# A gated mix of a recurrent memory attention and a full attention: paired weight tails, and attention steps set between the first products

## The chip, the cores and the metric

The kernel runs on one core of a Trainium2 chip, as one launch. The metric is device time in microseconds (us). TensorE is called PE, VectorE DVE, ScalarE ACT, GpSimd POOL; SP is the engine whose queue issues most of the transfers ("sync").

## The reference, cut to what matters

Two attentions over the same 2048 tokens of 576 features are mixed by a gate. A works in 64 segments of 32 tokens, each with 8 memory rows ahead of it. The memory of a segment is what the segment before gave out, so the segments of A form one long chain. B is an ordinary attention of 32 heads of 18 features over all tokens, without a mask, and depends on nothing in A.

```python
def A(x, mem, Wq, Wk, Wv, Wo):              # H, Dh = 32, 128; M, seg = 8, 32
    for s in range(64):
        h = concatenate([mem, x[:, 32*s:32*s+32]], axis=1)      # 40 rows
        q, k, v = h @ Wq, h @ Wk, h @ Wv                        # 576 -> 32 x 128 each
        scores = where(mask, q @ k.T * Dh ** -0.5, -1e9)
        o = (softmax(scores) @ v) @ Wo                          # 4096 -> 576
        mem = o[:, :8]
        outs.append(o[:, 8:])

def B(x, wqkv, wo):                         # 32 heads of 18
    q, k, v = split(x @ wqkv)
    return softmax(q @ k.T * 18 ** -0.5) @ v @ wo

g = sigmoid((x * gate_w).sum(-1))
out = g * A + (1 - g) * B
```

All tensors are bfloat16.

## The kernel before

The order of work on every engine is the order of the program. There are three parts: an opening (x is transposed, B's q, k and v are projected to DRAM, A's weights are loaded), the 64 segments, and a closing part (B's output product and the gate).

B's attention is cut into 512 steps (8 groups of four heads, 4 blocks of 512 queries, 16 blocks of 128 keys). A step is one PE part, `B` in the order strings below, and one exponential on ACT, `E`. The score tile `sb` has one buffer of four PSUM banks, so the scores of a step wait for the exponential of the one before.

```python
for j in range(4):                                   # scores: four row groups of PE, 32x128
    nc.tensor.matmul(sb[:, j, :], lhsT=kc[32*j:32*j+32, o:o+P],
                     rhs=qch[gq][32*j:32*j+32, :], tile_position=(32*j, 0), ...)
...                                                  # values of the step before: four column groups, 128x32
nc.scalar.activation(out=before, in_=sb, func=ACT.Exp, scale=scale_b)      # E, 128 x 2048
```

q and k of B lie in DRAM in the form in which the steps want them, 32 rows for a head of 18, so that one load brings a group. The 14 rows of padding are zeroed by transfers of their own, and a block of projected rows is stored head by head.

```python
qtd = dpool.tile([GB, P, S], BF16, name="qtd")       # ktd the same
def load_kv(g, kc):
    loads.dma_start(out=kch[g, kc][:, :], in_=ktd[g, :, kc*KC*P:(kc+1)*KC*P])
    ...
def store_qk(blk, groups):                           # one transfer for each head (or part of one) in the block
    while f < (blk + 1) * P: ... nc.sync.dma_start(out=(qtd, ktd)[which][h // 4, r:r+n, :], in_=stgs[blk][...])
```

The 576 features are four chunks of 128 and a tail of 64. The tails of a weight lie in two halves of one tile, one in each half of the partitions; the other half of the moving or stationary rows is zero, so a tail is multiplied as a full chunk of 128 rows. A segment's projection takes 32 tokens as stationary data and four column groups of PE at a time:

```python
def project(x, w, b, k):                             # Q0 Q1 K0 K1 V0 V1
    for c in range(NF + 1):                          # NF = 4; the fifth is the tail
        for j in range(4):
            rw, cc = w_slice(w, c, (2*(j//2)+b)*1024 + (j%2)*512, 512)
            nc.tensor.matmul(pv[32*j:32*j+32, :], lhsT=ht[:, cc, :], rhs=rw,
                             start=(c == 0), stop=(c == NF), tile_position=(0, 32*j))
```

A segment has 40 rows, `ht` has 32 columns: the last 8 tokens of the segments don't depend on the memory as queries, keys and values, and are projected for 16 segments at once (`last_tokens`, 24 pieces a group: q, k and v by eights). Group 0 is done ahead of the segments; groups 1 to 3 fill places `F0` to `F2` in segments 0 to 47, where every fourth segment uses these places for its group's output product instead. From segment 48 on there is none of it left.

Each segment's work is put in order by a string; names are steps, `B` and `E` halves of B's steps, `/` and `:` parts of B's divisions on DVE. `Q0` is a product, `cQ0` its copy out of PSUM, `tq0` transposes, `pq0` their copy, `S` scores, `x` their exponential, `n` the mask, `p` sums, `l` and `r` the reciprocal by logarithm and exponential, `m` the division, `w` and `o` values and their copy, `a` the output product, `h` and `g` its two bfloat16 halves, `f` and `ht` the fold into the next segment's `ht`.

```python
ORDERS = {
    7: "Q0 cQ0 K0 B E : cK0 / K1 tq0 tk0 pq0 V0 cK1 B E : pk0 Q1 S0 cV0 v0 cQ1 x0 tk1 n0 B E : ...",
    8: "Q0 B E : V0 cQ0 K0 cV0 v0 B / cK0 E : tq0 pq0 Q1 tk0 pk0 cQ1 B / E : S0 K1 tq1 x0 cK1 B ...",
}
eights = GB * NQC * NKB + 1 - done[0] - 7 * n_seg    # done: steps taken before the segments
width = 8 if s >= n_seg - eights else 7
```

In the opening, the steps are taken after whole products:

```python
def between(cost):
    spare[0] += cost
    if spare[0] >= 1.8:
        spare[0] -= 1.8
        b_advance(1)
for kb in range(NKB):
    project_vb(1, kb, 3)                             # second half of B's values, nine tiles in turn
for blk in (1, 6, 2, 7, 3, 8):
    for t in range(NQC):
        project_qk(blk, t, 0)                        # five matmuls of 512
        between(1.1)
    store_qk(blk, range(GB))
...                                                  # wo is loaded
for i, _ in enumerate(last_tokens(0, 1 << 30)):      # group 0: 24 pieces, four staging tiles
    if i % 2:
        between(1.1)
```

Of the kernel before, what the change touches and what calls it, by code (L numbers as in the profile page):

```python
# [16 lines left out]
def kernel(  # L17
# [64 lines left out]
    qtd = dpool.tile([GB, P, S], BF16, name="qtd")  # L82
    ktd = dpool.tile([GB, P, S], BF16, name="ktd")
# [11 lines left out]
    def weights(name):  # L95
        return (
            aw1.tile([P, NF, HD], BF16, name=name + "_m"),
            aw1.tile([P, HD // 2], BF16, name=name + "_t"),
        )

    wv, wq, wk = weights("wv"), weights("wq"), weights("wk")

    def load_weights(w, src):
        w2 = src.rearrange("d h e -> d (h e)")
        for c in range(NF):
            yield nc.gpsimd.dma_start(out=w[0][:, c, :], in_=w2[c * P:(c + 1) * P, :])
        for two in range(2):
            yield nc.gpsimd.dma_start(
                out=w[1][TL * two:TL * two + TL, :],
                in_=w2[NF * P:Dm, two * (HD // 2):(two + 1) * (HD // 2)],  # L110
            )

    def w_slice(w, c, f0, n):

        if c < NF:
            return w[0][:, c, f0:f0 + n], c
        f1 = f0 % (HD // 2)
        return w[1][:, f1:f1 + n], NF + f0 // (HD // 2)
# [17 lines left out]
    KC = 4  # L136
    last_stage = []
# [51 lines left out]
    def b_steps():  # L189


        kch, vch, qch = {}, {}, {}

        def load_kv(g, kc):
            kch[g, kc] = bint.tile([P, KC * P], BF16, name="kch", bufs=6)
            loads.dma_start(out=kch[g, kc][:, :], in_=ktd[g, :, kc * KC * P:(kc + 1) * KC * P])
            vch[g, kc] = bint.tile([P, KC * P], BF16, name="vch", bufs=6)
            first_loads[:] = [loads.dma_start(
# [4 lines left out]
        def load_q(i):  # L203
            if i < GB * NQC:
                g, qc = divmod(i, NQC)
                qch[i] = bint.tile([P, QC], BF16, name="qch", bufs=3)
                loads.dma_start(out=qch[i][:, :], in_=qtd[g, :, qc * QC:(qc + 1) * QC])
# [54 lines left out]
    loads, first_loads = nc.sync, []  # L262
# [30 lines left out]
    xlbs = {}  # L293
# [6 lines left out]
    def last_tokens(q, share, k=None):  # L300
# [3 lines left out]
        stage = (lambda: seg2.tile([P, 512], BF16, name="tm", bufs=4)) if share else (  # L304
            lambda: fil.tile([P, 512], BF16, name="vl")
        )
        store = nc.sync if share else nc.gpsimd
        xlb = xlbs.pop(q)
        for b in range(HD // 512):
            pv = bank(k[0], [P, 512], FP32, "pv")  # L310
            for c in range(NF + 1):
                rw, cc = w_slice(wv, c, b * 512, 512)
                nc.tensor.matmul(pv[:, :], lhsT=xlb[:, cc, :], rhs=rw, start=(c == 0), stop=(c == NF))  # L313
            vl = stage()
            yield
            copy_out(vl[:, :], pv[:, :], share)
            store.dma_start(out=vld[q * P:(q + 1) * P, b * 512:(b + 1) * 512], in_=vl[:, :])
            yield
        for w, dstd in ((wq, qld), (wk, kld)):
            for b in range(H // 4):  # L320
# [16 lines left out]
                if w is wk and b == H // 4 - 1:  # L337
                    load_xlb(q + 1)
                yield

# [34 lines left out]

    zt = pw.tile([P, S], BF16, name="stg", bufs=3)
    nc.vector.memset(zt[0:32 - DhB, :], 0.0)

    def pads(t, g):
        return t[g].rearrange("(j r) s -> j r s", r=32)[:, DhB:32, :]  # L380

# [33 lines left out]
    def project_qk(blk, t, share):  # L415
# [3 lines left out]
        for c in range(NF + 1):  # L419
# [6 lines left out]
            )  # L426
        copy_out(stgs[blk][:, t * QC:(t + 1) * QC], pq[:, :], share)

    def store_qk(blk, groups):
        f = blk * P  # L430
        while f < (blk + 1) * P:
            which, h, e = f // Dm, f % Dm // DhB, f % DhB
            n = min(DhB - e, (blk + 1) * P - f)
            r = 32 * (h % 4) + e
            if h // 4 in groups:
                nc.sync.dma_start(
                    out=(qtd, ktd)[which][h // 4, r:r + n, :], in_=stgs[blk][f - blk * P:f - blk * P + n, :]
                )
            f += n
# [18 lines left out]

    FIRST = (0, 4, 5)
    pieces = [(w, src) for w, src in ((wv, A_Wv), (wq, A_Wq), (wk, A_Wk))]  # L460
    pieces = (d for w, src in pieces for d in load_weights(w, src))
    for t in range(NQC):
        for n in range(4 * t, 4 * t + 4):
# [6 lines left out]
        if t == 0:  # L470
            load_xlb(0)
            for r in range(8):
                nc.gpsimd.dma_start(out=pads((qtd, ktd)[r // 4], 0)[r % 4], in_=zt[0:32 - DhB, :])
        for blk in FIRST:
            project_qk(blk, t, 2)
        if t == NQC - 1:
            for blk in FIRST:
                store_qk(blk, (0,))
        for kb in range(4 * t, 4 * t + 4):
            project_vb(0, kb, 2)  # L480

# [6 lines left out]
    load_first()  # L488
    ready.extend([first_loads[-1]] * 2)
# [19 lines left out]


    spare = [0.0]

    def between(cost):
        spare[0] += cost
        if spare[0] >= 1.8:
            spare[0] -= 1.8
            b_advance(1)

    for blk in FIRST:
        store_qk(blk, range(1, GB))  # L520
    for kb in range(NKB):
        project_vb(1, kb, 3)
    for blk in (1, 6, 2, 7, 3, 8):
        for t in range(NQC):
            project_qk(blk, t, 0)
            between(1.1)
        store_qk(blk, range(GB))
# [5 lines left out]
    for q in range(4):  # L533
        in_turn(
            nc.gpsimd.dma_start(
                out=wo[:, 8 * q:8 * q + 8, :], in_=A_Wo[8 * q:8 * q + 8].rearrange("h e d -> e h d")
            )
        )
    fix = actx.enter_context(tc.tile_pool(name="fix", bufs=1))
    seg2 = actx.enter_context(tc.tile_pool(name="seg2", bufs=2))  # L540


    def pad(g):
        for t in (qtd, ktd):
            nc.gpsimd.dma_start(out=pads(t, g), in_=pads(t, 0))

    pad(1)


# [582 lines left out]
```

The softmax here doesn't subtract the row's maximum and nothing guards it: scores larger than these inputs give would overflow.

## Time and profile before

| | |
|---|---|
| time, median of three runs | 1616.8 us (1615.98 to 1621.42) |
| span of the profiled execution | 1613.9 us |
| first product of the first segment | 174.5 us |
| PE, DVE, ACT, POOL busy | 91%, 59%, 71%, 21% of the span |
| PE on the chain that ended last | 69% |
| DMA, moved in all | 114.39 MB |

The busy share of PE counts each matmul from its start to its modelled end. As matmuls are pipelined, 379 ns of a matmul of 512 overlap with its neighbours, and the true cost of one is read from the distance of starts. The chain that ended last goes back from the last instruction to what released it, and names the engine that set the time at each moment; DMA has 4% of it, ACT and DVE 11% each. The most frequent line on it is the segments' projection with 27%.

### The profile page before, as it was taken

How to read it: one execution, taken by the hardware profiler on the slowest of the kernel's cores; microseconds unless marked ns; L12 is line 12 of the kernel's file. 1: busy time of each engine (PE TensorE's matmuls, PEld its weight loads, DVE VectorE, ACT ScalarE, POOL GpSimd, SP SyncE). 2: the span in 40 equal slices, each digit the busy share in tenths (PEclk: the TensorE clock that was granted, in tenths of full speed). 3: DMA queues.
4: the chain of work that ended last, by engine and by line, in shares of the span. 5: the costliest groups of instructions: out<-in, count | busy, mean ns of one | idle time of the engine just before them, and what ended most of it. 6: DMA issues, size and time to landing. Idle time of an engine off the chain costs nothing.

```text
span 1613.9 us, 57766 instructions
## 1 busy us (share of the span) xinstructions
PE 1476.7 (91%) x25082; PEld 782.0 (48%) x25082; DVE 960.0 (59%) x2355; ACT 1139.8 (71%) x981; POOL 338.4 (21%) x731
## 2 busy tenths in 40 slices
PE   6598899999999999999999999999999989998997
PEld 3434444555454444555454445555554444444445
DVE  2233666666566666666566666666666656565656
ACT  2165577777677767777677777777777777788774
POOL 6311211213131031302121211212121212120131
PEclk9899999999999999999999999999999999999999
DMA  7788322212122121212122121212221121211125
GB/s 200 235 291 290 100 65 64 49 42 52 45 50 53 32 53 38 61 36 49 43 43 60 38 50 40 57 39 45 51 53 35 30 48 34 45 34 35 29 59 162
DMA packets 209865, 114.39 MB, mean 71 GB/s; under 512 B 159491, under 2 KB 197251, under 8 KB 208019
## 3 DMA queue, kind: packets, MB, share of 16 engines
q1 hardware_dynamic: 188971, 58.40, 16.1%
q0 software_dynamic: 19696, 50.02, 9.9%
q8 instruction: 196, 3.21, 0.9%
q10 hardware_dynamic: 944, 2.29, 0.4%
q14 instruction: 58, 0.48, 0.1%
HBM read 60.94 MB, written 36.10 MB: 60 GB/s over the span
## 4 chain that ended last, share of the span: by engine, by line
PE 69%; ACT 11%; DVE 11%; DMA 4%; issue 2%; SPq 1%; POOL 1%; DVEq 0%; ACTq 0%; POOLq 0%
PE pvv L755 27%; ACT etb L257 9%; PE sb L238 8%; PE ob L222 7%; PE pt L782 5%; PE pv L326 4%; PE psh L800 3%; PE acc L643 3%; PE pso L838 3%; PE pv L313 2%; DVE hl L657 2%; PE pq L420 2%; DVE hl L654 2%; DVE ot L850 2%; ACT rq L830 2%
## 5 line engine op out<-in xcount | busy, mean ns | idle before, releaser
L257 ACT ACTIVATE etb<-sb 128x2048 bf16<-128x2048 f32 x512 | 959.6, 1874 | 341.9 <-PE sb L238 341.1
L767 DVE CAST tm<-pvv 128x512 bf16<-128x512 f32 x384 | 264.4, 689 | 175.1 <-PE pvv L755 174.2
L755 PEld LDWEIGHTS <-ht 128*32 128x32 bf16 x7680 | 185.8, 97 | 183.7 <-DVE ht L891 14.1
L238 PE MATMUL sb<-qch,kch 32*128 32x512 bf16 x2048 | 203.2, 386 | 38.5 <-ACT etb L257 36.7
L222 PE MATMUL ob<-etb,vch 128*32 128x512 bf16 x2048 | 205.9, 392 | 3.9 <-DVE tq L159 3.9
L850 DVE CAST ot<-pso 128x320 bf16<-128x320 f32 x256 | 120.7, 488 | 104.2 <-PE pso L838 99.9
L643 PE MATMUL acc<-wo,ot 128*32 128x384 bf16 (+1 forms) x4096 | 159.7, 291 | 5.4 <-DVE ot L850 3.3
L755 PE MATMUL pvv<-wq_m,ht 128*32 128x512 bf16 x2048 | 134.2, 382 | 13.0 <-DVE ht L891 8.3
L755 PE MATMUL pvv<-wk_m,ht 128*32 128x512 bf16 x2048 | 134.9, 384 | 0.0
L755 PE MATMUL pvv<-wv_m,ht 128*32 128x512 bf16 x2048 | 134.3, 382 | 0.0
L643 PEld LDWEIGHTS <-ot 128*32 128x32 bf16 x4096 | 105.2, 98 | 46.5 <-DVE ot L850 12.8
L700 POOL DMA_DIRECT2D a_dram<-rl x186 | 92.6, 506 | 162.4 <-DVE rl L695 143.3
L238 PEld LDWEIGHTS <-kch 32*128 32x128 bf16 x2048 | 61.2, 91 | 128.5 <-issue 107.9
L857 POOL COPY otl<-ot 128x256 bf16<-128x256 bf16 x64 | 25.9, 405 | 445.6 <-DVE ot L850 445.6
L222 PEld LDWEIGHTS <-vch 128*32 128x32 bf16 x2048 | 52.9, 93 | 120.6 <-issue 116.0
L782 PE MATMUL pt<-ident,tm 128*128 128x128 bf16 x1024 | 96.8, 221 | 0.8 <-DVE tm L767 0.8
L790 DVE COPY kt<-pt 128x512 bf16<-128x512 bf16 x128 | 54.0, 422 | 69.4 <-PE pt L782 69.0
L838 PE MATMUL pso<-et,v_sb 64*128 64x40 bf16 x2048 | 81.4, 178 | 14.9 <-DVE hll L657 4.7
L838 PEld LDWEIGHTS <-v_sb 64*128 64x128 bf16 x2048 | 62.8, 93 | 62.4 <-issue 49.5
L654 DVE CAST hl<-acc 128x384 bf16<-128x384 f32 (+1 forms) x128 | 57.9, 452 | 58.1 <-PE acc L643 57.8
L782 PEld LDWEIGHTS <-tm 128*128 128x128 bf16 x1024 | 57.8, 98 | 67.0 <-issue 49.4
L826 ACT ACTIVATE lt<-pss 128x320 f32<-128x320 f32 x128 | 56.0, 438 | 43.2 <-PE pss L822 32.8
(141 smaller groups left out, 1847.4 us busy)
## 6 DMA issues: line engine op xcount, KB each, us to landing
v_sb<-tm SPq DMA_DIRECT2D x512, 32.0 KB
wo<-in_A_Wo_dram POOLq DMA_DIRECT2D x4, 1152.0 KB, 9.7
wv_m<-in_A_Wv_dram POOLq DMA_DIRECT2D x4, 1024.0 KB, 8.0
wq_m<-in_A_Wq_dram POOLq DMA_DIRECT2D x4, 1024.0 KB, 9.1
wk_m<-in_A_Wk_dram POOLq DMA_DIRECT2D x4, 1024.0 KB, 8.0
xl<-qld SPq DMA_DIRECT2D x64, 64.0 KB
xl<-kld SPq DMA_DIRECT2D x64, 64.0 KB
v_sb<-vld SPq DMA_DIRECT2D x128, 32.0 KB
```

The source lines that it names most:

```text
L222: nc.tensor.matmul(ob[32 * j:32 * j + 32, :], lhsT=vc[:, o + 32 * j:o + 32 * j + 32], rhs=et4[:, j, :], start=(kb == 0), stop=(kb == NKB - 1),
L238: nc.tensor.matmul(sb[:, j, :], lhsT=kc[32 * j:32 * j + 32, o:o + P], rhs=qch[gq][32 * j:32 * j + 32, :], start=True, stop=True, tile_posi ...
L257: nc.scalar.activation(out=before[:, :, :], in_=sb[:, :, :], func=ACT.Exp, scale=scale_b)
L326: nc.tensor.matmul(pv[:, o:o + P], lhsT=lw, rhs=xlb[:, cc, :], start=(c == 0), stop=(c == NF))
L643: nc.tensor.matmul(acc[32 * j:32 * j + 32, 0:d1 - d0], lhsT=o[:, h, 0:CT], rhs=wo[:, h, d0:d1], start=(b == 0 and i == 0), stop=(b == 1 an ...
L654: nc.vector.tensor_copy(out=hl[:, 0, d0:d1], in_=acc[:, 0:d1 - d0])
L700: eng.dma_start(out=rows4[m, seg - LO:seg, i * n:(i + 1) * n], in_=rl[32 * i + m * LO:32 * i + (m + 1) * LO, :],)
L755: nc.tensor.matmul(pv[32 * j:32 * j + 32, :], lhsT=ht[:, cc, :], rhs=rw, start=(c == 0), stop=(c == NF), tile_position=(0, 32 * j),)
L767: nc.vector.tensor_copy(out=sbt[x][:, :], in_=ps[x][:, :])
L782: nc.tensor.transpose(out=pt[:, which, :, :, :].rearrange("p j (u i) t -> p j u i t", i=4)[:, :, :, i, :], in_=sbt[x][:, i * Dh:(i + 1) * Dh],
L838: nc.tensor.matmul(pso[:, i * L:(i + 1) * L], lhsT=v_sb[64 * jj:64 * jj + 64, b * 1024 + i * Dh:b * 1024 + (i + 1) * Dh], rhs=et[64 * jj:6 ...
L850: nc.vector.tensor_copy(out=ot[:, j * HG:(j + 1) * HG, :].rearrange("p h t -> p (h t)"), in_=ps["o", b, jj][:, 0:W8],)
```

## The change

It does six things. The tails of the weights are laid out so that the tails of two products lie in different halves of the partitions, and three steps `T0`, `T1` and `T2` multiply them in pairs, each with 64 rows, in eight tiles of PE at once; the first four chunks stay as they were. The last 16 segments, which have no last-token work, keep whole projections and the old eight-step order. The other segments have new orders, and those with eight steps are the first ones now. Last-token values and the sums of the softmax are computed in four column groups. q and k of B lie densely in DRAM, without padding, and are loaded head by head into tiles that were zeroed once; blocks are stored whole. In the opening, steps are set between the matmuls of a product, last-token pieces alternate with products, part of the weights is loaded earlier and `wo` later.

The purpose is to give PE less to do where it is full, and to keep it supplied in the opening.

```diff
-    qtd = dpool.tile([GB, P, S], BF16, name="qtd")
-    ktd = dpool.tile([GB, P, S], BF16, name="ktd")
+    qkd = dpool.tile([2 * Dm, S], BF16, name="qkd")
...
+    wv, wq, wk = weights("wv", 1), weights("wq", 1), weights("wk", 0)     # which half holds the odd quarters
...
+        def load_heads(eng, t, f, t0):
+            for j in range(4):
+                eng.dma_start(out=t[32 * j:32 * j + DhB, :], in_=qkd[f + j * DhB:f + (j + 1) * DhB, t0:t0 + QC])
...
-    def store_qk(blk, groups):
-        ... (a transfer for each head)
+    def store_qk(blk):
+        nc.sync.dma_start(out=qkd[blk * P:(blk + 1) * P, :], in_=stgs[blk][:, :])
...
+    for t in range(NQC):
+        for _ in range((0, 1, 1, 2)[t]):
+            next(pieces)                        # weight pieces; order wq, wk, wv (was wv, wq, wk)
...
+    first_tokens = last_tokens(0, 1 << 30)
+    def some_tokens():
+        for _ in range(2):
+            next(first_tokens, None)
+        between(1.1)
-    for kb in range(NKB):
+    for kb in range(NKB // 2):
         project_vb(1, kb, 3)
-    for blk in (1, 6, 2, 7, 3, 8):
+    for i, blk in enumerate((1, 6, 2, 7, 3, 8)):
         for t in range(NQC):
             project_qk(blk, t, 0)               # calls between(.22) after each matmul; a step at 1.7
-            between(1.1)
-        store_qk(blk, range(GB))
+            if i > 0:
+                some_tokens()
+            else:
+                for kb in range(NKB // 2 + 2 * t, NKB // 2 + 2 * t + 2):
+                    project_vb(1, kb, 3)
+        store_qk(blk)
...
+        def project_tails(two):
+            two = [(x, w, b, begin(x)) for x, w, b in two]
+            for j in range(4):
+                for x, w, b, first in two:
+                    t, r = w_tail(w, columns(b, j), 512)
+                    nc.tensor.matmul(ps[x][32 * j:32 * j + 32, :], lhsT=ht[TL * r:TL * r + TL, NF + r, :],
+                                     rhs=t[TL * r:TL * r + TL, :], start=first, stop=(not first),
+                                     tile_position=(TL * r, 32 * j), ...)
...
+        if not whole:
+            step("T0", project_tails, (("Q0", wq, 0), ("K0", wk, 0)))
+            step("T1", project_tails, (("Q1", wq, 1), ("K1", wk, 1)))
+            step("T2", project_tails, (("V0", wv, 0), ("V1", wv, 1)))
...
     ORDERS = {
-        7: (as above)
+        7: """
+        Q0 T0 B E : cQ0 K1 K0 B Q1 cK0 T1 tq0 cK1 tk0 pk0 E : pq0 B E : cQ1 V0 S0 x0 T2 cV0 v0 B V1 n0
+        p0 tq1 tk1 E : cV1 v1 B l0 E : pk1 / pq1 F1 S1 x1 r0 cF1 F2 n1 m0 p1 l1 w01 B cF2 w00 r1 o01 m1
+        o00 w11 o11 w10 a00 o10 ol E : a01 h0 a10 a11 B F0 g0 f0 h1 g1 E : cF0 f1 ht0 ht1 og oh / /
+        """.split(),
         8: """
+        Q0 B T0 K1 E : / cQ0 T1 cK1 B Q1 E : K0 B V0 cQ1 cK0 T2 tk0 E : tq0 B V1 / cV0 v0 pk0 E : pq0
+        tk1 tq1 cV1 v1 pq1 S0 pk1 B x0 / F1 E : n0 S1 p0 x1 cF1 n1 l0 F2 p1 r0 m0 w00 B cF2 l1 o00 r1 F0
+        m1 w01 w11 cF0 o01 E : w10 o11 o10 ol a00 B a01 E : a10 h0 a11 B g0 h1 f0 g1 ht0 f1 ht1 E : og
+        oh
+        """.split(),
+        0: (the old 8, with whole projections)
...
-    eights = GB * NQC * NKB + 1 - done[0] - 7 * n_seg
+    wides = GB * NQC * NKB + 1 - done[0] - 7 * n_seg - SG
...
-        width = 8 if s >= n_seg - eights else 7
+        width = 8 if s < wides else 7 if s < n_seg - SG else 0
```

`SG` is 16. The order of the PSUM banks is new as well for widths 7 and 8.

## The prediction

> **What bounds the kernel now.** I read the granted clock first (0.986 over the span, 0.99 to 1.00 in the segments: no throttling to explain), then the forty slices, the stages, the order of TensorE's work inside one segment, and last the waits of the opening. The stages come from the four-stage table; its borders are the first and last writes of the memory columns of `ht` (197.3 and 1558.0) and the first segment products (174.5).
>
> ```profile
> PE   6598899999999999999999999999999989998997
> 0.00:174.50 174.50, 130.37 (x1110) 72.33 (x1110) 62.08 (x118) 72.97 (x82) 53.42 (x106) 0.93 0.77 244
> 197.30:787.90 590.60, 555.50 (x10044) 297.04 (x10044) 374.84 (x930) 419.47 (x352) 121.71 (x266) 0.99 0.21 50
> 787.90:1212.60 424.70, 409.67 (x7274) 213.76 (x7274) 266.24 (x668) 326.73 (x266) 86.83 (x190) 1.00 0.21 47
> 1212.60:1558.00 345.40, 314.98 (x5742) 160.38 (x5743) 210.17 (x537) 274.55 (x225) 55.87 (x130) 1.00 0.17 35
> ```
>
> After the borders and the length the columns are the busy time of PE, weight loads, DVE, ACT and POOL, then clock, DMA share and GB/s. Rows two to four are 27 segments of seven attention steps (21.87 us each), 19 of eight with last-token work beside them (22.35) and 16 of eight without it (21.59). PE is busy 94%, 96% and 91% of them, ACT 71%, 77% and 79%, DVE about 62%. So PE's queue sets the length of the first two kinds. The third has less PE work and is hardly shorter: there the segment's own chain and the exponentials count too. What PE does is seen in the order of time:
>
> ```profile
> 700.38 1.05 PE L755 MATMUL pvv<-wq_m,ht 128*32 128x512 bf16 x16
> 701.25 0.39 PE L755 MATMUL pvv<-wq_t,ht 128*32 128x512 bf16 x4
> 701.47 1.04 PE L755 MATMUL pvv<-wk_m,ht 128*32 128x512 bf16 x16
> 702.33 0.39 PE L755 MATMUL pvv<-wk_t,ht 128*32 128x512 bf16 x4
> 702.65 0.40 PE L238 MATMUL sb<-qch,kch 32*128 32x512 bf16 x4
> 702.98 0.40 PE L222 MATMUL ob<-etb,vch 128*32 128x512 bf16 x4
> 703.20 1.04 PE L755 MATMUL pvv<-wk_m,ht 128*32 128x512 bf16 x16
> ```
>
> Read starts, not durations. Four column-tiled matmuls of 512 start together and occupy PE for 0.22 us (701.25 to 701.47; the fifth chunk, a tail of 64 rows padded with zeros, costs as much as a full one). From the tails to the scores it is 0.32 us (702.33 to 702.65), from scores to values 0.33, from values to the next products, which keep the tile shape, 0.22. A change of tile shape thus costs 0.1 us.
>
> The opening waits for data instead:
>
> ```profile
> PE pvb L447 <- DVE xn L291: 16.0, 1, 16.0
> PE sb L238 <- ACT etb L257: 5.0, 10, 0.5
> PE pvb L447 <- DVE stg L291: 4.4, 1, 4.4
> PE pq L420 <- DMA wb<-in_B_wqkv_dram: 3.9, 4, 2.0
> PE ob L222 <- DVE tq L159: 3.9, 1, 3.9
> PE ptm L616 <- DVE ht L598: 3.2, 1, 3.2
> ```
>
> The 16 us are from 62.9 to 78.84: the value tiles can't be reused before their stores land, and these stand in the sync queue behind the many small stores of q and k by head, while A's weights fill the DMA engines:
>
> ```profile
> 66.00:150.00 84.00, 62.63 (x438) 27.14 (x438) 29.47 (x49) 40.68 (x24) 13.98 (x24) 0.88 0.88 296
> 63.44 2.85 SPq L436 DMA_DIRECT2D qtd<-stg  x8
> 66.34 2.75 SPq L436 DMA_DIRECT2D ktd<-stg  x7
> 69.32 5.61 SPq L455 DMA_DIRECT2D vgd<-xn  x5
> ```
>
> **What the Trainium skill says.** "TensorEngine Tiling (Array Packing)", section Key Properties: changing the tiling mode drains TensorE. The trace agrees, with 0.1 us. "TensorE: Matmul & The Clock Gate", section Part 3: Packing small matmuls: tiles that differ in rows and columns run together, at about 4 ns more per tile. The trace agrees for four tiles; no run yet shows eight tiles of 64x32, on which the pairing rests. "DMA: Bandwidth & Descriptors", section Issuing engines are not separate DMA queues: sync and gpsimd transfers share 16 engines, so a second issuing queue saves issue time only. The 0.88 share above, with gpsimd's weights and sync's stores together, agrees; hence it helps that fewer stores are issued and that `wo` comes later, not who issues.
>
> **The change, part by part.** First the counts. Attention steps before the segments: formerly 48 calls of 1.1 against 1.8, so 29; now 24x5 calls of 0.22 and 24 of 1.1, together 52.8 against 1.7, so 31. The rest of 513 gives 513-31-448-16 = 18 wide segments at the start, then 30 of seven steps, then 16 of the old eight-step order with whole projections (formerly 28 and 36).
>
> (a) Tails. Each segment had six tail groups of four, 6x0.215 = 1.29 us. T0, T1 and T2 do eight matmuls each in the two row halves; if those run together that is 3x0.215 = 0.645. Saved 0.645 in 48 segments.
>
> (b) Shape changes. Going through the order strings and counting neighbours of different shape (B counts as two shapes), a seven-step segment had 28 to 31 and has 27 to 29, though each T adds up to two, because T sits next to a step, the sums are now column-tiled, and last-token values keep the 128x32 shape. An eight-step one had 32 to 34 and has 30 to 33. Over the four kinds of segments in a group (two last-token fills in three of them, group output in one) that is about 2 and 2.5 changes, 0.2 and 0.25 us.
>
> (c) New waits. I walked the new orders with the rows' durations: 0.69 for a copy out of `pvv`, 0.42 for `qt` and `kt`, 1.88 for an exponential, 0.43 to 0.47 for the three small activations. The first steps are 2.25 to 2.35 us apart on PE, just what scores plus exponential need; the second half waits for the exponentials about as now. The walk gave some 20.4 and 21.1 us, but such a walk leaves out small queue gaps, so I credit only (a) and (b): 21.87-0.85 = 21.02, and 22.35-0.9 = 21.45. The last 16 keep their order and gain only 0.1: 21.49.
>
> (d) Opening, now 174.5 us. In PE's timeline the gate sums end at 55.4; eight value products of the second pass (7.51 us for 12, 0.63 each) bring it to 60.4. The first attention loads need the three stores; I add 4 us for their landing: 64.4. Then, all from the same timeline, 24 products of 1.17 (2.33 for two), eight value products of 0.63, 24 last-token products of 1.17 (2.34 for two) and 31 steps of 0.66 (0.33 twice): 28.1+5.0+28.1+20.5 = 81.7, so 146. The even spacing (eight matmuls of 0.22 and a step, 2.4 us) leaves no exponential wait; 2 us remain for odd waits: 148. The 16 us wait goes since eight tiles are used before the stores must land and 15 further stores no longer stand ahead; the 9.2 us for `qld` stores (151.75 to 160.93 in the chain of waits) since there are five stages and a product between; the 5 us of setup (169.6 to 174.5 in the chain: `cap`, `bsel`, `sel`, `ht`) since `sel`, `ht` and the memory are ready earlier. Four weight pieces move into the first 50 us, where DMA was busy 63 to 79%; the other 14 need some 50 us at the old pace and end near 115, before their last-token values start.
>
> (e) Loads of q and k by head: 57 gpsimd issues become 228, 171 more of about 0.55 us, 94 us on POOL (the rows of today's `qch` and `kch` issues have 548 and 545 ns), whose 338 busy us are 21% of the span. POOL is off the path unless a blocked load delays the `qt` and `kt` copies; I count nothing. The closing loads are issued a little elsewhere, but behind the same sync queue (until 1573.8): nothing.
>
> Sum: 148 + 18x21.45 + 30x21.02 + 16x21.49 + 34.3 for the closing part (55.9 less one segment of 21.6) = 148+386+631+344+34 = **1543 us**, 4.5% less.
>
> **Rivals.** *The pairs don't overlap*: T then costs 0.43 each, (a) falls away in 48 segments, 31 us: about 1574. Against it: scores, tiled in four row groups into four banks, already run at full speed (0.32 with the shape change), and each pair here writes two banks. *The chain becomes the bound*: tails now come after the main products, and copies, transposes and scores start later; the 16 segments without last-token work stay at 21.5 with 2 us less PE work, which says the chain is not far away. If wide segments can't go below 22 and narrow ones below 21.6: 18x0.55+30x0.6 = 28 us back, 1571. *POOL or the loads stall*: in the table of waits POOL already waited 44 us, seven times, for `kch` buffers; if each of 28 key loads cost 1 us on the path, 1571. *The opening stays bound by DMA*: half its gain lost, 1556. On the other side, the walk's 20.4 and 21.1 would bring 1518.
>
> **Range and chances.** One rival alone lands near 1570, two near 1600; the walk lowers it to 1518. So 1512 to 1580, with faster by over 2% (below 1584.5) 0.88, within 2% 0.09, slower 0.03.
>
> **What would show it.** Starts of T groups: 0.32 us to the next shape if pairs overlap, over 0.5 if not. The first segment products near 148, with no wait above 5 us after 60. 18 segments near 21.4, 30 near 21.0, the rest unchanged. PE waits in segments still led by the exponential; if `ht`, `kt` or POOL lead, the order cost more than it saved. It would be wrong if segments keep their length while PE's busy share falls.

## The result and the profile after

| | before | changed |
|---|---|---|
| time, median (lowest to highest), us | 1616.7 (1616.0 to 1621.4) | 1571.9 (1570.7 to 1572.5) |
| ratio, 95% interval | | 0.972 (0.970 to 0.974) |
| span of the profiled execution, us | 1613.9 | 1570.6 |
| first product of the first segment, us | 174.5 | 148.5 |
| from there to the end, us | 1439.4 | 1422.1 |

The kernel gains 45 us, and the prediction had 1543 us, some 74 less than before. The prediction adds up stages, so it is compared with the spans (43 us gained of 71). The opening gave the 26 us it was to give. The segments and the closing part gave 17 us where the prediction has 44, so the missing 27 us are nearly all in the segments. First, in the page of the changed kernel, the slices of PE (each digit tenths of 39.3 us):

```profile
PE   7899999999999999999999999999988899998997
```

The hole in the opening (6 and 5 in the first two slices before) is gone, and the rest looks as full as it was. So a view by stage is needed. The first border is the first product of the first segment, the others are the first copy of the new memory into `ht`, 0.2 to 1.2 us ahead of the segment's first product; the rows are the opening, the first segment, the 17 other wide ones, the 30 narrow ones, 15 of the last 16, and the last one with the closing part. The columns are those of the stages shown of before.

```profile
0.00:148.50 148.50, 127.54 (x1231) 71.30 (x1250) 61.23 (x124) 75.27 (x85) 53.81 (x105) 0.99 0.74 244
148.50:174.60 26.10, 22.69 (x388) 12.06 (x381) 13.25 (x30) 18.10 (x15) 11.53 (x24) 0.93 0.76 244
174.60:547.00 372.40, 355.12 (x6704) 191.23 (x6705) 238.94 (x593) 296.57 (x239) 93.50 (x202) 1.00 0.20 45
547.00:1188.40 641.40, 602.96 (x11550) 321.00 (x11549) 407.55 (x1033) 462.53 (x391) 178.91 (x386) 0.99 0.21 45
1188.40:1514.20 325.80, 299.39 (x5486) 152.56 (x5486) 196.85 (x506) 257.29 (x211) 66.75 (x151) 0.97 0.17 33
1514.20:1570.60 56.40, 45.76 (x582) 28.39 (x581) 33.52 (x78) 31.89 (x46) 12.06 (x23) 0.93 0.49 148
```

| stage | predicted, us | measured, us | difference |
|---|---|---|---|
| opening | 148 | 148.5 | +0.5 |
| first segment | 21.45 | 26.1 | +4.6 |
| 17 wide segments | 364.7 (21.45 each) | 372.4 (21.91) | +7.7 |
| 30 narrow segments | 630.6 (21.02) | 641.4 (21.38) | +10.8 |
| 15 of the last 16 | 322.4 (21.49) | 325.8 (21.72) | +3.4 |
| last segment and closing part | 55.8 | 56.4 | +0.6 |

PE is still busy 95% of the wide segments and 94% of the narrow ones, as before. That share can't tell what bounds them: a segment's matmul of 512 columns is recorded with 381 ns in the mean, while undivided ones (128x128) follow each other every 216 ns, so the record covers idle time behind a matmul as well. The waits of PE in the opening, in us in total, times and longest:

```profile
PE sb L261 <- ACT etb L280: 4.7, 7, 1.0
PE pq L442 <- DMA wb<-in_B_wqkv_dram: 4.3, 2, 2.4
PE ptx L421 <- DMA xn<-in_A_x_dram: 3.6, 1, 3.6
...
PE pvb L461 <- DVE xn L314: 2.1, 1, 2.1
```

The 16.0 us of `pvb` behind the value tiles have become 2.1 us, and no single wait is above 3.6 us. The chain that ended last, by engine:

```profile
PE 58%; ACT 18%; DVE 11%; DMA 5%; issue 3%; POOL 3%; SPq 3%; ACTq 0%; DVEq 0%; POOLq 0%
```

PE had 69% of it and ACT 11%. The changed kernel's chain runs through the exponential more often, and POOL, which the prediction counted as nothing, is on it with 3%. Both are followed up below. Now PE in a wide segment, in order of time:

```profile
307.72 0.40 PE L261 MATMUL sb<-qch,kch 32*128 32x512 bf16 x4
308.04 0.40 PE L245 MATMUL ob<-etb,vch 128*32 128x512 bf16 x4
308.38 0.39 PE L825 MATMUL pvv<-wq_t,ht 64*32 64x512 bf16 x1
308.38 0.39 PE L825 MATMUL pvv<-wk_t,ht 64*32 64x512 bf16 x1
...
308.40 0.39 PE L825 MATMUL pvv<-wk_t,ht 64*32 64x512 bf16 x1
308.71 1.05 PE L810 MATMUL pvv<-wk_m,ht 128*32 128x512 bf16 x16
```

All eight matmuls of `T0` start between 308.38 and 308.40, and the next shape starts at 308.71. The pair costs 0.33 us, shape change included. Over all 144 such groups the medians are 0.02 us from the first start to the last and 0.34 to the next shape. So the pairs do run together. And ACT in another wide segment, where the number in brackets is the idle time before an instruction:

```profile
354.63 1.88 ACT L280 ACTIVATE etb<-sb 128x2048 bf16<-128x2048 f32 x1 [0.56 <-PE sb L261]
357.07 1.88 ACT L280 ACTIVATE etb<-sb 128x2048 bf16<-128x2048 f32 x1 [0.56 <-PE sb L261]
359.50 1.88 ACT L280 ACTIVATE etb<-sb 128x2048 bf16<-128x2048 f32 x1 [0.56 <-PE sb L261]
...
362.09 1.88 ACT L280 ACTIVATE etb<-sb 128x2048 bf16<-128x2048 f32 x1
...
366.80 1.86 ACT L280 ACTIVATE etb<-sb 128x2048 bf16<-128x2048 f32 x1
369.18 1.88 ACT L280 ACTIVATE etb<-sb 128x2048 bf16<-128x2048 f32 x1 [0.53 <-PE sb L261]
371.61 1.88 ACT L280 ACTIVATE etb<-sb 128x2048 bf16<-128x2048 f32 x1 [0.56 <-PE sb L261]
```

Read the starts: 2.43 us apart, again and again. That is the closed loop of `sb`: 1.88 for the exponential, and 0.55 until the next scores have let the next one start. The small activations of the segment stand where lines are left out: one between 359.50 and 362.09, five between 362.09 and 366.80, a stretch of 4.71 in which ACT idles for only 0.6. From 349.77, two steps ahead of the first line, to 371.61 there are eight steps: five of 2.43, and 2.59, 4.71 and 2.38, in all 21.84 us. That is a whole wide segment (21.91 in the mean).

My theory after this view: in the wide segments PE's queue and the loop of the exponential end together, so PE work saved no longer shows. In the narrow ones either the same holds, or POOL holds them up. The rivals are a cost of the new orders themselves, the loads by head, and a plain shift of the bound to the exponential alone.

### The profile page after: what moved, and what is told of

It reads as the page before. It is cut to its first block, busy times and chain, and to the rows that moved or that the text cites. A ratio compares the mean times of both kernels' runs of the same rounds, so it can differ in the third digit from the quotient of the medians.

```text
span 1570.6 us, 59696 instructions
## 1 busy us (share of the span) xinstructions
PE 1453.5 (93%) x25931; PEld 776.5 (49%) x25946; DVE 951.3 (61%) x2361; ACT 1141.6 (73%) x983; POOL 416.6 (27%) x890
## 4 chain that ended last, share of the span: by engine, by line
PE 58%; ACT 18%; DVE 11%; DMA 5%; issue 3%; POOL 3%; SPq 3%; ACTq 0%; DVEq 0%; POOLq 0%
PE pvv L810 17%; ACT etb L280 14%; PE sb L261 9%; PE ob L245 6%; PE pt L852 4%; PE pv L337 3%; PE acc L687 3%; PE psh L870 3%; DMA v_sb<-tm 3%; POOL a_dram L744 2%; SPq L842 2%; DVE ot L928 2%; PE pq L442 2%; PE pvv L825 2%; PE pv L354 2%
## 5 line engine op out<-in xcount | busy, mean ns | idle before, releaser
L810 PEld LDWEIGHTS <-ht 128*32 128x32 bf16 x6528 | 163.2, 97 | 151.6 <-DVE ht L969 11.6
L687 PE MATMUL acc<-wo,ot 128*32 128x384 bf16 (+1 forms) x4096 | 156.0, 296 | 3.5 <-DVE ot L928 0.3
L935 POOL COPY otl<-ot 128x256 bf16<-128x256 bf16 x64 | 25.7, 402 | 421.0 <-DVE ot L928 421.0
L261 PEld LDWEIGHTS <-kch 32*128 32x128 bf16 x2048 | 68.7, 91 | 127.7 <-issue 102.9
L810 PE MATMUL pvv<-wk_m,ht 128*32 128x512 bf16 x2048 | 127.9, 380 | 0.0
L687 PEld LDWEIGHTS <-ot 128*32 128x32 bf16 x4096 | 99.0, 99 | 45.0 <-DVE ot L928 16.3
L852 PE MATMUL pt<-ident,tm 128*128 128x128 bf16 x1024 | 85.2, 221 | 0.0
L870 PEld LDWEIGHTS <-kt 128*64 128x64 bf16 x2048 | 61.5, 112 | 41.1 <-issue 14.1
L904 ACT ACTIVATE lt<-pss 128x320 f32<-128x320 f32 x128 | 55.7, 435 | 33.5 <-PE pss L893 31.8
```

The lines of the kernel that those rows point to most:

```text
L261: nc.tensor.matmul(sb[:, j, :], lhsT=kc[32 * j:32 * j + 32, o:o + P], rhs=qch[gq][32 * j:32 * j + 32, :], start=True, stop=True, tile_posi ...
L687: nc.tensor.matmul(acc[32 * j:32 * j + 32, 0:d1 - d0], lhsT=o[:, h, 0:CT], rhs=wo[:, h, d0:d1], start=(b == 0 and i == 0), stop=(b == 1 an ...
L810: nc.tensor.matmul(ps[x][32 * j:32 * j + 32, :], lhsT=ht[:, cc, :], rhs=rw, start=(first and c == 0), stop=((whole or not first) and c == ...
L852: nc.tensor.transpose(out=pt[:, which, :, :, :].rearrange("p j (u i) t -> p j u i t", i=4)[:, :, :, i, :], in_=sbt[x][:, i * Dh:(i + 1) * Dh],
L870: nc.tensor.matmul(psh[64 * jj:64 * jj + 64, i * L:(i + 1) * L], lhsT=kt[:, h * L:h * L + 64], rhs=qt[:, h, :], start=True, stop=True, til ...
```

## The experiments

All ratios are to the kernel before. Segment lengths are means in us; "narrow" is segments 18 to 27 and, where given, all of 18 to 47.

| kernel | time, us | ratio (95%) | wide, 1 to 17 | 18 to 27 | 18 to 47 in all |
|---|---|---|---|---|---|
| before | 1616.7 | | 21.86 (old seven-step order) | 21.91 | |
| changed | 1571.9 | 0.972 (0.970 to 0.974) | 21.91 | 21.10 | 641.4 |
| opening only | 1584.0 | 0.979 (0.977 to 0.981) | 21.80 (old seven-step order) | 21.61 | |
| no pairs | 1579.2 | 0.976 (0.974 to 0.977) | 22.49 | 21.22 | 641.1 |
| half exponentials, changed | 1554.1 | 0.960 (0.958 to 0.962) | 21.37 | 20.89 | 640.0 |
| half exponentials, before | 1598.6 | 0.988 (0.985 to 0.990) | 21.52 (old seven-step order) | 21.45 | |
| no tails | 1552.9 | 0.958 (0.954 to 0.961) | 21.98 | 20.63 | 628.3 |
| no tails, half exponentials | 1497.9 | 0.924 (0.920 to 0.928) | 20.18 | 19.94 | 605.3 |
| one load for four heads | 1569.2 | 0.968 (0.964 to 0.971) | 21.86 | | 642.6 |
| small stores by halves | 1561.1 | 0.963 (0.961 to 0.966) | 21.92 | 21.01 | 634.2 |
| small stores on sync | 1564.0 | 0.966 (0.964 to 0.968) | 21.94 | | 636.4 |
| by halves, `wo` on sync | 1573.4 | 0.972 (0.969 to 0.975) | 21.91 | 21.38 | 641.4 |
| by halves, again | 1560.0 | 0.964 (0.962 to 0.966) | 21.92 | | 635.3 |
| changed, again | 1572.7 | 0.972 (0.970 to 0.974) | 21.96 | | 644.2 |

### The opening alone, and the orders without pairs

The first kernel keeps the new opening, the dense q and k and the loads by head, but has the old orders with whole projections, and values and sums in the old 128x128 form.

```diff
-        width = 8 if s < wides else 7 if s < n_seg - SG else 0
+        width = 0 if s >= n_seg - SG - wides else 7     # ORDERS and BANKS of before
-            for j in range(4): nc.tensor.matmul(pv[32*j:32*j+32, :], lhsT=xlb[:, cc, 32*j:32*j+32], ...)
+            nc.tensor.matmul(pv[:, :], lhsT=xlb[:, cc, :], rhs=rw, start=(c == 0), stop=(c == NF))
```

> The changed kernel's opening and its loads by head, with the segments as before (old orders, whole projections, values and sums not column-tiled, wide segments last; 34 wide ones instead of 36). Theory: the opening alone brings some 26 us and the loads by head cost nothing with the old orders: first segment product at about 148 us, time about 1588 us, ratio 0.982. Rival (loads by head hold up POOL and so the segments): 1600 us or more, with narrow segments over 22.1 us. Rival (opening is worth less once its transfers are pushed into the first segments): first product near 148, but a first segment over 26 us, about 1593 us.

The second has the new orders but leaves out the `T` steps, with each product multiplying its own tail again.

```diff
-        todo = segment(s, BANKS[width], "T0" not in ORDERS[width])
-        for name in ORDERS[width]:
+        todo = segment(s, BANKS[width], True)
+        for name in [n for n in ORDERS[width] if n[0] != "T"]:
```

> The changed kernel with its new orders, but every projection whole: the steps T0, T1 and T2 are left out and each product multiplies its tail as a fifth chunk. Theory (in wide segments the loop scores, exponential, scores sets the pace, in narrow ones PE does): narrow segments 0.6 to 0.85 us longer, wide ones at most 0.3 us longer, together 20 to 30 us: 1592 to 1602 us, ratio 0.985 to 0.991. Rival (pairs are worth the same in all 48 segments): 31 to 40 us, 1603 to 1612 us. Rival (shape changes around T eat up what pairs save): within 5 us of 1572.

The opening alone brought 2.1%, more than expected: besides the 27 us of the opening the kernel has two wide segments fewer, and its end is 2 us shorter. The new orders without pairs, together with values and sums in four column groups, brought another 0.3%, and the pairs another 0.4%. The two kinds of segments behaved the other way round from what I had expected. The stages of the kernel without pairs, the 17 wide and the 30 narrow segments:

```profile
170.80:553.20 382.40, 356.55 (x6705) 194.56 (x6703) 238.48 (x593) 296.60 (x239) 93.48 (x202) 1.00 0.20 44
553.20:1194.30 641.10, 604.75 (x11549) 326.32 (x11549) 409.45 (x1032) 464.02 (x391) 178.99 (x386) 1.00 0.21 45
```

Pairs save 10.0 us in the 17 wide segments (0.59 each) and nothing in the 30 narrow ones (641.4 with them, 641.1 without). So of the 48 segments in which (a) was credited, 30 gave no return. The stores that are found below don't hide one: in the 22 narrow segments that don't begin behind a group's output, the changed kernel takes 467.4 us (466.1 in its second profile) and this one 468.8, at most 0.1 us a segment.

Even in the wide segments the gain doesn't look like work that PE no longer does: PE's recorded busy time differs by 1.4 us there, and its wait for the exponential by 10.9. In the kernel without pairs that wait is:

```profile
PE sb L261 <- ACT etb L280: 16.6, 34, 0.7
```

In the changed kernel it is 5.7 us.

### Is it the exponential?

Here only half of each score tile is exponentiated; the other half of the exponential tile holds a constant 1. One exponential takes 1.02 us in place of 1.88. This leaves out half of B's exponentials, in the changed kernel and in the one before.

```diff
-                before = bint.tile([P, 4, QC], BF16, name="etb", bufs=2)
-                nc.scalar.activation(out=before[:, :, :], in_=sb[:, :, :], func=ACT.Exp, scale=scale_b)
+                before = ets[(NKB * gq + kb) % 2]        # two tiles, set to 1.0 once
+                nc.scalar.activation(out=before[:, 0:2, :], in_=sb[:, 0:2, :], func=ACT.Exp, scale=scale_b)
```

> The changed kernel with each large exponential over half of its 2048 columns; the other half of the weights is a constant, so half of B's softmax is left out. PE's work stays. Theory: with exponentials of about 1.02 us the loop of a step falls from 2.43 to 1.6 us, wide segments fall from 21.9 to about 20.2, the last 16 from 21.7 to about 20, narrow ones by under 0.7 us: about 1500 us. Rival (PE's own work with its shape changes fills wide segments): wide segments stay above 21.5 us, time above 1550 us.

> The kernel before with the same shortened exponentials. Theory: the change is worth more where the loop does not bind, so this kernel stays 60 us or more above the changed one with short exponentials: about 1565 us, wide segments with last-token work about 21.3 us. Rival (loop has no part in the missing gain): the distance stays at 45 us.

The theory behind these two kernels fell. Nearly half of ACT's work in B was taken away, and each kernel became only 18 us faster (19 and 20 by the ratios): the two stay 44.5 us apart, as with whole exponentials. The exponential alone doesn't hold the changed kernel. The narrow segments hardly noticed:

```profile
175.50:538.80 363.30, 351.19 (x6702) 184.69 (x6698) 237.28 (x593) 180.77 (x239) 93.64 (x202) 1.00 0.21 46
538.80:1178.80 640.00, 601.94 (x11549) 315.92 (x11549) 408.26 (x1033) 289.54 (x391) 179.01 (x386) 0.98 0.21 45
```

ACT's busy time (fourth of the busy columns) fell from 462.53 to 289.54 us in the 30 narrow segments, and their length by 1.4 us.

### Tails away, and both

Next the tails were left out altogether (the last 64 of 576 features of the segments' products), in all but the last 16 segments, and then the tails and half of the exponentials together.

```diff
-                        stop=((whole or not first) and c == n - 1),
+                        stop=(c == n - 1),
-        for name in ORDERS[width]:
+        for name in [n for n in ORDERS[width] if n[0] != "T"]:
```

> The changed kernel with the tails of the six products left out altogether in the first 48 segments (no T steps and no fifth chunk; each product sums 512 of the 576 features); the exponentials are whole. It takes 0.65 us of matmuls and 0.3 to 0.4 us of shape changes from PE in each of these segments. Theory (in narrow segments PE's order, the loop of 2.43 us a step and the closing chain from the sums to the next Q0 end nearly together, so taking from one brings little): narrow segments at most 0.4 us shorter, wide ones about 0.5 us: 1550 to 1558 us. Rival (PE's work alone is the bound in 48 segments): 0.95 us each, about 1526 us.

> The same without tails, and with the large exponentials over half of their columns as well. Theory (two limits that nearly coincide): the two cuts together bring clearly more than the sum of each alone; with 18 us for the exponentials and some 18 for the tails that sum is 36 us (1536 us), and I expect 1505 to 1520 us. Rival (each cut takes its own separate waits): 1536 us. Rival (closing chain alone sets narrow segments): about 1540 us, narrow ones not under 20.4 us.

In their times both kernels did what the theory of coinciding limits expects; only the wide segments without tails were to be 0.5 us shorter and are not. Half exponentials brought 18 us alone and no tails 19, 37 in sum, but both brought 74 together. First the stages without tails, wide and narrow, then those of both:

```profile
170.90:544.50 373.60, 336.57 (x6298) 186.41 (x6296) 238.26 (x594) 296.68 (x239) 93.54 (x202) 1.00 0.20 44
544.50:1172.80 628.30, 573.03 (x10829) 311.55 (x10828) 408.94 (x1033) 462.69 (x391) 178.98 (x386) 0.99 0.21 46
```

```profile
175.10:518.10 343.00, 331.13 (x6294) 179.82 (x6292) 236.55 (x594) 180.74 (x239) 93.82 (x202) 1.00 0.22 48
518.10:1123.40 605.30, 566.35 (x10829) 303.80 (x10829) 408.59 (x1034) 288.30 (x391) 179.05 (x386) 0.99 0.22 48
```

Compare the wide rows with 372.40 of the changed kernel. Without tails PE's busy time falls by 18.5 us and the length rises by 1.2. The time reappears as PE's wait for the exponential. The waits of PE in the wide segments, first of the changed kernel and then of the one without tails:

```profile
PE sb L261 <- ACT etb L280: 5.7, 17, 0.3
```

```profile
PE sb L261 <- ACT etb L280: 25.1, 51, 0.9
```

It rose by 19.4 us, the whole of what was taken away. With half exponentials as well the same segments lose 29.4 us. So with paired tails the wide segments stand where PE and the loop of the exponential meet. In the narrow ones half exponentials bring 1.4 us, no tails 13.1, and both together 36.1, so there too the two limits lie close together. A third may lie beside them, the segment's closing chain. It is read from the chain of the changed kernel: from `pss` at 668.97 through the two small activations, the division, `pso`, `ot`, `acc` and its halves to the first product of the next segment at 675.03, it is 6.1 us in which every piece waits for the one before. No kernel shortens this chain, so its part isn't shown, and how much each of the three holds in which narrow segment wasn't separated.

### Is it the loads by head?

Four loads by head become one load of the dense rows, so that the operands of a group are no longer in their row groups (the values of B's scores then differ; the work on PE and ACT is the same).

```diff
-            for j in range(4):
-                eng.dma_start(out=t[32*j:32*j+DhB, :], in_=qkd[f+j*DhB:f+(j+1)*DhB, t0:t0+QC])
+            n = min(P, 2 * Dm - f)
+            eng.dma_start(out=t[0:n, :], in_=qkd[f:f+n, t0:t0+QC])
```

> The changed kernel with each q and k tile of B loaded by one transfer of 128 dense rows in place of four of 18 rows: the rows then don't stand where the heads want them, so B is computed on wrong rows, with the same work on every engine. Takes 171 issues of 0.51 us from POOL in the segments. Theory (POOL's issues delay the copies of the last tokens into qt and kt, and hold up DVE and PE behind them): the segments 18 to 47 fall from 21.4 to about 21.1 us, the waits of DVE for POOL's kt copies vanish, about 1563 us. Rival (POOL is off the path): within 3 us of 1572.

It made no difference that can be told: 0.968 (0.964 to 0.971) against 0.972 (0.970 to 0.974), with overlapping intervals. POOL's busy time in the narrow segments falls from 178.9 to 135.6 us, their length not at all (642.6 us). The rival named in the theory is out. But one wait of DVE stayed what it was. In the narrow segments, of the changed kernel and then of this one:

```profile
DVE kt L860 <- POOL kt L1134: 7.2, 7, 3.2
```

```profile
DVE kt L858 <- POOL kt L1132: 7.4, 7, 3.4
```

Seven times DVE waits for a copy on POOL, at the start of segment 46 for 3.2 and 3.4 us, the six other times for some 0.66. What keeps POOL busy there is seen in its order of time in segment 46 of the changed kernel:

```profile
1141.33 0.52 POOL L744 DMA_DIRECT2D a_dram<-rl  x1 [3.24 <-DVE ht L971]
1142.08 3.47 POOL L744 DMA_DIRECT2D a_dram<-rl  x7 [0.23 <-issue]
1147.94 1.99 POOL L744 DMA_DIRECT2D a_dram<-rl  x4 [2.40 <-issue]
1149.92 0.32 POOL L599 COPY ht<-xg 128x144 bf16<-128x144 bf16 x1
1150.51 0.40 POOL L1134 COPY kt<-xl 128x256 bf16<-128x256 bf16 x1
```

Twelve small stores of a group's output stand on POOL from 1141.33 to 1149.92, and only then come the copies that the segment needs. The stores themselves take 6.0 us of it. The other 2.6 are gaps in which POOL waits for nothing that the profile shows. Behind the six other outputs there is no such gap, and why segment 46 has one is open. The new narrow order does that output product last (`F0`, `cF0` at the end of the string), so that these stores stand straight ahead of the next segment's copies. The kernel before issued them earlier. Its segment 46 has its first product at 1191.0, and the twelve stores are done by then but for 0.9 us:

```profile
1185.97 5.97 POOL L700 DMA_DIRECT2D a_dram<-rl  x12 [19.08 <-DVE et L833]
1194.51 0.40 POOL L1059 COPY kt<-xl 128x256 bf16<-128x256 bf16 x1
```

There the copy of `kt` starts 3.5 us after the segment's first product, in the changed kernel 9.3. In the whole profile of the kernel before DVE waits for that copy once, for 0.4 us, so the wait is new. A group's output comes in every fourth segment; seven of the narrow ones begin behind one (22, 26 and so on to 46).

### The small stores moved

Half of these stores go to the sync queue, as was done already in the last segment.

```diff
-                eng = nc.sync if s3 == n_seg - 1 and m % 2 else nc.gpsimd
+                eng = nc.sync if m % 2 else nc.gpsimd
```

> The changed kernel with half of the twelve small stores that follow every fourth segment's last rows issued from the sync queue instead of gpsimd (3 us less of POOL in every fourth segment). Theory (POOL's queue is what delays the copies at a boundary of B's groups): 3 to 6 us less than 1572. Rival (sync is as full, and delays the value stores): no less, or up to 5 us more.

> The kernel with half of the stores from sync once more, beside the two others on the same chip: 1561 us as the first time, if the gain over 1572 is that of the stores.

> The changed kernel itself on the same chip, as the base of the three others: 1572 us, ratio 0.972.

Beside each other, the changed kernel took 1572.7 us (1570.9 to 1576.5) and this one 1560.0 (1558.2 to 1563.7), 0.964 of the kernel before (0.963 the first time). That is twice the 3 to 6 us expected. The same place in its segment 46:

```profile
1134.54 3.01 POOL L744 DMA_DIRECT2D a_dram<-rl  x6 [3.22 <-DVE ht L971]
1137.54 0.32 POOL L599 COPY ht<-xg 128x144 bf16<-128x144 bf16 x1
1138.13 0.40 POOL L1134 COPY kt<-xl 128x256 bf16<-128x256 bf16 x1
```

Six stores take 3.0 us, here without a gap, and DVE's wait for POOL's `kt` copy no longer appears. In these two profiles the narrow segments fall from 644.2 to 635.3 us; segment 46 alone falls from 25.7 to 20.9, and the six others behind a group's output by 0.4 in the mean. POOL is gone from the chain:

```profile
PE 61%; ACT 18%; DVE 11%; DMA 5%; issue 3%; SPq 2%; ACTq 0%; DVEq 0%
```

With the two earlier profiles (641.4 and 634.2) the narrow segments lose 8 us in the mean, about half of it in segment 46. The times fall by 11 to 13 us. The 3 to 5 us beyond the narrow segments lie in the opening in one pair of profiles and in the last segments and the closing part in the other, so they can't be given to one place.

Two variants asked whether more is to be had. In one all the stores go to sync; in the other half of them do, and `wo` is loaded from sync as well, to take POOL's wait out of the first segment.

```diff
-                eng = nc.sync if s3 == n_seg - 1 and m % 2 else nc.gpsimd
+                eng = nc.gpsimd if s3 == n_seg - 1 and m % 2 else nc.sync
```

> The changed kernel with all twelve small stores of every fourth segment issued from the sync queue (in the last group half of them from gpsimd). If POOL's queue is what these stores block, a further 0 to 4 us less than with half of them moved: 1558 to 1562 us. If the sync queue is the next to fill, the value stores and the next segment's loads stand behind twelve issues of 0.3 to 0.5 us, and the time goes back to 1565 us or more.

```diff
-            nc.gpsimd.dma_start(out=wo[...], in_=...)
+            nc.sync.dma_start(out=wo[...], in_=...)
```

> Half of the small stores from sync as before, and the four loads of wo from the sync queue instead of gpsimd. In the changed kernel POOL waits 12.4 us for them while it issues the next key loads, and the first segment takes 26.0 us instead of about 22. If the queue is the reason, the first segment falls to 23 us and the time to about 1558 us. If it is the bytes (4.7 MB on the shared DMA engines beside the value stores), the first segment stays at 25 to 26 us and the time at 1561.

All stores on sync is 1564.0 us (1563.2 to 1564.5), not clearly apart from the halves (0.966 against 0.964, the intervals overlap). With `wo` on sync the whole gain is lost, which neither theory expected: 1573.4 us. Its first segment takes 34.8 us, 9 to 10 us more than in the kernel with the stores by halves. (Its narrow segments take 641.4 us. Segment 46 stays short with 21.3, but 24 and 32 take 24.3 and 23.4, each 2.6 to 3.3 us more than by halves, and the cause of that is open.) The waits of PE and of DVE in it, then the sync queue:

```profile
PE pvv L825 <- DVE tm L837: 11.1, 1, 11.1
```

```profile
DVE tm L837 <- DMA vld<-tm: 14.7, 1, 14.7
```

```profile
143.04 6.86 SPq L643 DMA_DIRECT2D wo<-in_A_Wo_dram  x4
149.95 3.21 SPq L655 DMA_DIRECT2D xl<-qld  x1
153.21 3.22 SPq L655 DMA_DIRECT2D xl<-kld  x1
156.47 3.01 SPq L365 DMA_DIRECT2D vld<-tm  x1
```

Four `wo` issues hold the queue for 6.9 us, two loads behind them for 6.4, and the value stores that must free the staging tile `tm` are issued only at 156.47. PE waits for them. An issue of `xl` takes 0.53 us in the median of the same trace, so behind `wo` these two take six times as long.

## Why the prediction was right, and where it was wrong

**The opening (d) was right**, in the sum and in its terms: 148.5 us for 148, the first scores at 64.14 where the first loads were to have landed at 64.4, the 16 us of the value stores down to 2.1, setup and `qld` waits gone. Among PE's waits in the opening there is none for the weights' pieces.

**(a) was right as work on PE.** Eight tiles start within 0.02 us, and the stretch to the next shape is 0.33 us, as the prediction's last part asked for. The first rival is out.

**(b) was nearly right as a count, and credited to the wrong part.** Counted in the traces, a seven-step segment has 28.8 shape changes in the mean before and 27.4 now, an eight-step one 33.5 and 30.9: 1.4 and 2.6 fewer, for 2 and 2.5 predicted. But without pairs the same orders have 24.4 and 27.0. So the `T` steps add three changes in a narrow and four in a wide segment, at 0.1 us each, and a pairing is worth 0.35 and 0.25 us of PE, not 0.645. In the wide segments it brought 0.59, more than that. With whole tails in these orders a copy out of PSUM also comes later, which may be the rest; that wasn't tried by itself. In the narrow segments it brought nothing. That these nonetheless got shorter by 0.49 us (21.87 to 21.38) is luck for the sum. Without pairs they take 21.37, so it was the rest of the change (the order, and sums and values in four column groups), not the tails, to which (a) had credited three quarters of the gain.

**(c) is the step that failed**: "I credit only (a) and (b)", with no new wait. The walk of the orders had the first steps 2.25 to 2.35 us apart; they are 2.43 apart, 1.88 for the exponential and 0.55 for scores and the way back. The trace of before already has this distance where one step follows another at once:

```profile
898.53 1.88 ACT L257 ACTIVATE etb<-sb 128x2048 bf16<-128x2048 f32 x1 [0.85 <-PE sb L238]
900.96 1.88 ACT L257 ACTIVATE etb<-sb 128x2048 bf16<-128x2048 f32 x1 [0.56 <-PE sb L238]
```

From 898.53 to 922.61, in eight-step segments of before, three of nine distances are 2.43 to 2.45 and the others 2.51 to 3.18; in the wide segment of the changed kernel five of eight are 2.43. That puts the wide segments on the loop of the exponential at 21.9 us: 0.46 above the 21.45 predicted, 7.7 us for seventeen. The second rival, "the chain becomes the bound", named almost this sum (22 and 21.6, 1571 us). That it hit the measured time within 1 us is partly luck: it puts 28 us into these 48 segments, where 23 were missing, and of these 4.6 belong to the first segment and some 8 to the stores on POOL. Its mechanism is only part of it. There isn't one new bound. PE and the loop end nearly together, in the narrow segments perhaps with the closing chain, and so taking work from PE alone brings little: pairs 0 in the narrow segments, leaving all tails out 0 in the wide ones.

**(e) was wrong as to POOL, but not for the reason that its rival gave.** The loads by head cost nothing that can be seen. What cost some 8 us in the narrow segments, most of their excess of 10.8, was the place of twelve small stores that the change left as they were and that its new order moved against the next segment's copies. The step "POOL is off the path unless a blocked load delays the `qt` and `kt` copies" had the right victim and named the wrong blocker. Nor did the prediction's "not who issues" hold for these stores: moving six of twelve to sync takes 3 us of issuing from POOL at each output, and with copies waiting behind it the kernel gained 11 to 13 us.

**Two smaller terms.** The first segment was counted like any other and took 23.8 to 26.6 us in the kernels with the changed opening, whole exponentials and `wo` on POOL. `wo` is now loaded beside it: in the changed kernel POOL waits there four times for `wo` transfers, 12.4 us in all, and PE for `v_sb` 2.4 us. Moving the issue to sync made it worse; whether the bytes or the queue are to blame in the changed kernel is open. The last 16 segments were predicted to gain 0.1 us, from 21.59 to 21.49, and didn't: their means lie between 21.52 and 21.73 in the ten profiles with the changed opening and whole exponentials. No kernel here tests that difference.

## What to carry to other kernels

Before crediting work taken from the busiest engine, compute the closed loops beside it (here scores, exponential, scores) to 0.1 us from the trace; where two limits lie within a few per cent, halve both in one run and each alone, and compare the sum (here 18 and 19 us alone, 74 together). When an order of work is rewritten, look at what every engine taken to be idle now does just ahead of the next round's first copy, also for operations that the change doesn't touch. Before a transfer moves to another queue, look at what will stand behind it there (here the stores that free `tm`).

## What the runs showed of the hardware

- Eight matmuls of 64x32 tiles, 512 columns each and into two banks, start within 0.02 us and cost 0.33 us with the shape change (0.34 in the median of 144 groups). Four tiles of 32x128 with the change cost 0.32.
- The way round the loop costs 0.55 us beyond the exponential: about 0.50 from the first scores matmul to the start of the exponential (307.72 to 308.22), and 0.05 from its end to the next scores. An exponential of 128x2048 takes 1.88 us, of 128x1024 1.02.
- A small store issued by POOL holds it for 0.5 us each (3.01 us for six, 3.47 for seven), and copies behind it wait. On sync the same stores take 0.29 us each in the median.
- The time of an issue isn't fixed. On sync the four of `wo` took 6.86 us together, the first 0.38 and the fourth 3.57, and the two of `xl` behind them 3.2 each, where the median in the same trace is 0.53.
